# Linear and multi-query attention, forward and gradient: where padding is zeroed, how a column of k sums is spread, and how the last dK products are placed

## The chip, the cores and the metric

The kernel runs on one core of a Trainium2 chip. Its time is the device time of one execution in microseconds, taken as the median of several runs. The profile is that of one further execution. Five engines work side by side, each with its own queue of instructions in a fixed order: TensorE (PE, with its weight loads shown apart as PEld), VectorE (DVE), ScalarE (ACT), GpSimd (POOL) and SyncE (SP). ACT, POOL and SP also issue DMA transfers from their queues, so an instruction that waits holds up the transfers behind it.

## What is computed

The reference joins two attention blocks side by side, on sequences of 2048 with 448 features and 16 heads of 28, and returns the output together with the gradients of all eight inputs. The kernel therefore computes a forward and a backward pass of both:

```python
def _A_ref(x, wqkv, wo):                      # linear attention
    q, k, v = heads(x @ wqkv)                 # (1, 16, 2048, 28) each
    phi = lambda t: jnp.where(t > 0, t + 1, jnp.exp(t)) + 1e-6
    pq, pk = phi(q), phi(k)
    kv = jnp.einsum("bhsd,bhse->bhde", pk, v)
    z = jnp.einsum("bhsd->bhd", pk)           # the sums over k
    num = jnp.einsum("bhqd,bhde->bhqe", pq, kv)
    den = jnp.einsum("bhqd,bhd->bhq", pq, z)[..., None] + 1e-6
    return merge(num / den) @ wo

def _B_ref(x, wq, wk, wv, wo):                # softmax attention, one k and one v for all heads
    q, k, v = heads(x @ wq), x @ wk, x @ wv
    p = softmax(jnp.einsum("bhqd,bkd->bhqk", q, k) * Dh ** -0.5)
    return merge(jnp.einsum("bhqk,bkd->bhqd", p, v)) @ wo

_out, _vjp = jax.vjp(forward, A_x, A_wqkv, A_wo, B_x, B_wq, B_wk, B_wv, B_wo)
return (_out, *_vjp(grad_out))
```

(`heads` and `merge` stand for the reshapes and transposes of the reference, which are cut here.)

## The kernel before

The sequence is cut into 16 tiles of 128 rows, the features into chunks of 128, 128, 128 and 64 rows. Everything is held in SBUF between the stages. There are three stages.

**Phase A, the linear attention** (`phase_A`), with its order made by a scheduler that interleaves what the code writes one after the other. It uses PSUM tiles of two names, four buffers each: "agen" for short products and "aacc" for accumulators. Its short-lived SBUF tiles come from the pool `awk` under three names: "osb" (three buffers, evicted results on their way to an output), "phiT" (three) and "pr" (two, f32).

- K, V and the k sums: `k1acc` collects x^T phi(k) over the tiles, and since columns 448 to 463 of x are ones (line 151), its rows 64 to 79 of chunk 3 hold the k sums. `hilo` (line 246) splits it into two bf16 parts `K1T`, line 284 transposes them by DMA into `K1`, and line 287 keeps the negated sums by head in `zrow`. Line 355 takes the column of sums out of the transposed `K1`, spreads it over the heads and masks it: `Zm`, which `den` (line 328) multiplies with phi(q).
- The gradient of wqkv: `gw` (line 429) accumulates x^T g over all tiles into four aacc banks, ACT copies three of them into osb tiles (line 444), ACT and DVE add the two halves of the fourth (lines 441 and 442, the sum in a fourth osb tile), and POOL issues the stores (line 445). It is called at line 450 and again at line 520.
- Between lines 419 and 427 the transposed weights `wqT` and `wkT` are brought by DMA, and POOL zeroes the unused half of their last chunk (line 422, "MEMSET ga"). POOL's queue holds this beside its copies of line 426, the stores of `gw` and the zeroing of `wo_pr` (line 467).
- After the first `gw` a product over the 16 tiles (lines 451 to 457) fills agen tiles that DVE evicts (line 457); POOL's and SyncE's loads for the next stage follow it. The loop of line 477 writes two outputs for each of four chunks through osb tiles (lines 481 and 491). The last product of the phase (line 525) needs `gkT`, which SyncE transposes at line 476.

**The main loop** (lines 911 to 1021) has its order written out by hand: `manual_schedule`, 512 steps u and 28 to empty the pipeline. A step computes two tiles of scores S (`rows_SD`), their exponentials (lines 940 and 986), dP (banks `DB`), dS (lines 952 to 955), and some steps later O and dQ (`o_dq`), dV (`dv_mm`) and dK (`dk_m`, line 855). A `dk_m` call issues four matmuls of 32x32 weights and 512 columns, on the four array tiles of the diagonal, (32a, 32a), into the one bank `dk_acc`. At odd u four of them are issued together. From u = 512 on there are no more scores; in the steps that remain, inputs of the drain are loaded (`post_load`, line 757), the gradient of wo is accumulated in spare banks (`gwo`, line 781, at even u from 520), and the last two tiles of the output projection are done (u = 532 and 536, in the bank `spare`). `post_load(8)` brings the padded weight `wqT`, and POOL then issues 14 small transfers that patch rows of it (`PADS`, line 770). At u = 531 SyncE transposes the finished dQ into `dqn`, in a tile of the name dsx (line 1011).

**The drain** (from line 1036), again ordered by the scheduler. dV and dK are copied into `dkvT` (lines 1036 to 1044; ACT and DVE take turns for dK), 14 small transfers patch rows of dQ^T (`qT_B`) with rows of `dkvT`, shared between SyncE and POOL (line 1083), `dwq` and `dkv_T` prepare weight gradients, and `dx` (line 1071) multiplies the patched dQ^T with the patched `wqT`. Results leave through `sbuf()`, a ring of five tiles of the name dsT.

Of the kernel before, what the change touches and what calls it, by code (L numbers as in the profile page):

```python
# [14 lines left out]
H = 16  # L15
# [10 lines left out]
def kernel(  # L26
# [61 lines left out]
    def flat(t):  # L88
        return t.rearrange("p a b -> p (a b)")
# [34 lines left out]
    def phase_A(pa, cA, cB, awk, psA):  # L124
# [157 lines left out]
        hilo(K1T, k1acc)  # L282
        for i in range(2):
            nc.sync.dma_start_transpose(K1[i][:].rearrange("p c h k -> p (c h) k"), flat(K1T[i]))
        for st in range(NS - LAG, NS):
            qproj(st)
        nc.vector.tensor_tensor(out=zrow[64:80, :], in0=k1acc[3][64:80, :], in1=mrow[64:80, :], op=ALU.mult)
# [67 lines left out]
        nc.vector.tensor_tensor(out=Zm[:], in0=hm[:], in1=K1[0][:, 3, :, 64:65].to_broadcast([P, 4, H]), op=ALU.mult)  # L355
# [65 lines left out]
        for t in (wqT, wkT):  # L421
            nc.gpsimd.memset(t[64:128, 3, :], 0.0)
# [6 lines left out]
        def gw(gn, blk):  # L429
# [6 lines left out]
            for c in range(4):  # L436
                r = DC_ROWS[c]
                sb = awk.tile([P, 512], BF16, name="osb")[:, 0:D]
                if c == 3:
                    odd = awk.tile([P, H, DH], F32, name="pr", bufs=2).rearrange("p h e -> p (h e)")[0:64, :]  # L440
                    nc.scalar.activation(out=odd, in_=al[3][64:128, :], func=ACT.Copy)
                    nc.vector.tensor_tensor(out=sb[0:64, :], in0=al[3][0:64, :], in1=odd, op=ALU.add)  # L442
                else:
                    nc.scalar.activation(out=sb[0:r, :], in_=al[c][0:r, :], func=ACT.Copy)
                g_ = nc.gpsimd.dma_start(out_2[c * P:c * P + r, blk * D:(blk + 1) * D], sb[0:r, :])
# [4 lines left out]
        gw(gqn, 0)  # L450
# [26 lines left out]
        for i in range(4):  # L477
# [13 lines left out]
            sb = awk.tile([P, 512], BF16, name="osb")[:, 0:D]  # L491
# [155 lines left out]
    with ExitStack() as cs_:  # L647
# [109 lines left out]
        def post_load(k):  # L757
# [8 lines left out]
            if k == 8:  # L766
                post["wqT"] = t[:, 0:4 * D].rearrange("p (g c) -> p g c", c=D)
                nc.sync.dma_start(post["wqT"], wqT_d[:, :].rearrange("(g p) c -> p g c", p=P))
                for g, r, c in PADS:
                    nc.gpsimd.dma_start(post["wqT"].rearrange("(j r) g c -> j r g c", r=32)[:, r, g, :], wkvT_d[c:c + 4, :])  # L770
# [24 lines left out]

        GW = [0, 0, 4, 4, 10, 10, 16, 16, 22, 22, 28, 28, 34, 34, 40, 40, 48, 48, 56, 56, 64, 64]
# [58 lines left out]
        def dk_m(b, m):  # L855
            qc, pair, g, hp = blk(b)
            h, B, s = m // 8, (m // 2) % 4, m % 2
            for a in range(4):
                rhs = dsx[b][32 * a:32 * a + 32, :, h, :, :].rearrange(
                    "p u t (b i s) -> p u t b i s", b=4, s=2)[:, :, :, B, :, s]  # L860
                mmt(dk_acc[32 * a:32 * a + 32, :],
                    qX[qc][32 * a:32 * a + 32, B, s, pair * 64 + 32 * h:pair * 64 + 32 * h + 32],
                    rhs, (32 * a, 32 * a), b == 0 and m == 0, b == NB - 1 and m == 15)
# [47 lines left out]
        with tc.manual_schedule():  # L911
# [8 lines left out]
            for u in range(NU + 28):  # L920
# [5 lines left out]
                spare = SB[(2 * u + 2) % 3] if hasS else SB[2]  # L926
# [66 lines left out]
                if u % 2:  # L993
                    b, i = divmod(u - 27, 8)
                    if 0 <= b < NB:
                        for m in range(2 * i, 2 * i + 4):
                            dk_m(b, m)
# [7 lines left out]
                if 512 <= u < 530 and u % 2 == 0:  # L1005
                    post_load((u - 512) // 2)
                if u == 531:
                    dqn = px_.tile([P, 8, 2, 2, 256], BF16, name="dsx").rearrange("p a b c d -> p (a b c d)").rearrange(
                        "p (t d) -> p t d", d=512)
                    for g_ in range(4):  # L1010
                        nc.sync.dma_start_transpose(dqn[:, :, g_ * P:(g_ + 1) * P], qT_B[g_])
# [24 lines left out]
        for c in range(4):  # L1036
            nc.vector.tensor_copy(out=dkvT[32:64, c * 512:(c + 1) * 512], in_=dv_acc[32 * c:32 * c + 32, :])
        for c in range(4):
            t = dkvT[0:32, :].rearrange("p (t a i) -> p t a i", a=4, i=32)[:, :, c, :]
            src = dk_acc[32 * c:32 * c + 32, :].rearrange("p (t i) -> p t i", i=32)  # L1040
            if c % 2:
                nc.vector.tensor_scalar(out=t, in0=src, scalar1=scale, scalar2=None, op0=ALU.mult)
            else:
                nc.scalar.activation(out=t, in_=src, func=ACT.Copy, scale=scale)

        def dwq(c):
            r = DC_ROWS[c]
            al = gen(0)
            for st in range(NS):
                rhs = dqn[:, st, :].rearrange("p (h c) -> p h c", c=32)[:, :, 1:1 + DH]  # L1050
# [84 lines left out]
```

## Time and profile before

| what | value |
|---|---|
| runs | 1065.06, 1064.52, 1064.60 us; median 1064.6 us |
| profiled execution | 1065.64 us, of which span 1063.9 us |
| busy: PE | 1013.7 us (95% of the span) |
| busy: DVE | 899.6 us (85%) |
| busy: ACT | 869.6 us (82%) |
| busy: POOL | 781.7 us (73%) |
| mean granted clock of TensorE | 0.998 |

The span is the stretch from the first to the last instruction in the profile; the run's time includes what lies around it. A busy share is a mean over the stages, and a PE shown as busy is not PE at its peak. A line of the order of time gives start, duration, engine, source line, operation, what it writes and reads, and in brackets how long its engine idled before it and who ended that. Inside a helper every matmul has the helper's line (81 for `mm`, 672 for `mmt`, 85 for `half_mm`), so the tile names tell which product it is.

The page's rows by slices of the span (40 equal ones, busy in tenths) show where the engines pause:

```
PE   9999799998999999999999999999999999999998
DVE  6897410569999999999999999999999999999942
ACT  6463032589999999999999999999999999999522
POOL 6001152228898998899889988989998988888881
```

### The profile page before, as it was taken

What the parts mean: (1) busy time and instruction counts of PE and PEld (TensorE: products, weight loads), DVE (VectorE), ACT (ScalarE), POOL (GpSimd) and SP (SyncE); (2) the same over time, 40 slices, a digit from 0 to 9 for tenths busy, and PEclk for the clock granted to TensorE, in tenths of its full rate; (3) what the DMA queues carried; (4) which work ended last, traced back from release to release, by engine and by line L of the source; (5) the groups of instructions that cost most, each with busy time, mean ns of one, the idle gap of its engine ahead of it and who ended that gap; (6) DMA issues with size and microseconds to landing.
All of it is one profiled execution on the core that took longest, in us unless ns stands there. A gap on an engine that the chain in (4) does not pass through costs nothing.

```text
span 1063.9 us, 40030 instructions
## 1 busy us (share of the span) xinstructions
PE 1013.7 (95%) x16232; PEld 487.2 (46%) x16241; DVE 899.6 (85%) x1799; ACT 869.6 (82%) x1739; POOL 781.7 (73%) x1034
## 2 busy tenths in 40 slices
PE   9999799998999999999999999999999999999998
PEld 5555355434444444444444444444444444444444
DVE  6897410569999999999999999999999999999942
ACT  6463032589999999999999999999999999999522
POOL 6001152228898998899889989988998989888881
PEclk9999999999999999999999999999999999999999
DMA  9879899179999999999999999999999999999963
GB/s 263 152 128 188 165 210 233 36 138 200 192 184 196 192 186 196 199 185 177 207 195 192 185 201 189 191 199 198 193 190 179 200 186 193 202 187 178 228 135 89
DMA packets 689937, 195.15 MB, mean 183 GB/s; under 512 B 670616, under 2 KB 687792, under 8 KB 689752
## 3 DMA queue, kind: packets, MB, share of 16 engines
q1 hardware_dynamic: 680152, 179.92, 101.9%
q0 software_dynamic: 4640, 8.71, 2.9%
q10 hardware_dynamic: 4960, 3.96, 1.3%
q8 instruction: 127, 2.08, 0.8%
q14 instruction: 58, 0.48, 0.2%
HBM read 12.60 MB, written 10.84 MB: 22 GB/s over the span
## 4 chain that ended last, share of the span: by engine, by line
PE 44%; ACT 32%; issue 13%; DVE 4%; POOL 4%; DMA 2%; ACTq 0%; DVEq 0%; SPq 0%; POOLq 0%
ACT cp L954 16%; ACT eT L986 13%; PE agen L81 12%; PE agen L672 11%; PE aacc L672 10%; PE aacc L81 7%; POOL dsT L955 3%; PE aacc L806 2%; ACT eT L940 2%; PE aacc L837 1%; DVE dsx L1019 1%; DVE dsT L952 1%; DMA dsx<-R 1%; DMA pk<-in_B_x_dram 1%; DMA out_dram<-osb 1%
## 5 line engine op out<-in xcount | busy, mean ns | idle before, releaser
L955 POOL TENSOR_TENSOR dsT<-cp,eT 128x512 bf16<-128x512 bf16 x512 | 588.3, 1157 | 77.0 <-ACT cp L954 70.6
L1019 DVE STREAM_TRANSPOSE dsx<-dsT 128x512 f32<-128x512 f32 x512 | 357.8, 699 | 4.1 <-POOL dsT L955 1.9
L672 PEld LDWEIGHTS <-R 32*128 32x128 bf16 (+1 forms) x9104 | 227.7, 94 | 275.4 <-issue 239.7
L952 DVE TENSOR_TENSOR dsT<-agen,eT 128x512 bf16<-128x512 f32 x512 | 341.9, 668 | 10.5 <-PE agen L672 5.4
L940 ACT ACTIVATE eT<-aacc 128x512 bf16<-128x512 f32 x512 | 313.1, 612 | 15.3 <-PE agen L672 6.0
L954 ACT ACTIVATE cp<-agen 128x512 bf16<-128x512 f32 x512 | 314.8, 615 | 12.6 <-PE agen L672 11.2
L986 ACT ACTIVATE eT<-aacc 128x512 bf16<-128x512 f32 x512 | 320.8, 627 | 0.0
L672 PE MATMUL agen<-dsx,qX 32*32 32x512 bf16 x4096 | 267.7, 375 | 0.0
L672 PE MATMUL agen<-doT,R 32*128 32x256 bf16 x2048 | 246.7, 269 | 3.0 <-DVE dsT L952 1.4
L672 PE MATMUL aacc<-R,R 32*128 32x256 bf16 (+1 forms) x2240 | 218.1, 268 | 8.1 <-DVE oTs L816 3.2
L672 PE MATMUL agen<-eT,R 128*32 128x256 bf16 x2048 | 158.0, 274 | 0.2 <-issue 0.2
L672 PE MATMUL agen<-dsT,R 128*32 128x256 bf16 x2048 | 157.0, 274 | 0.1
L672 PEld LDWEIGHTS <-qX 32*32 32x32 bf16 x4096 | 79.7, 89 | 113.9 <-issue 53.3
L672 PE MATMUL aacc<-eN,don 128*32 128x512 bf16 x1024 | 96.9, 379 | 0.0
L81 PEld LDWEIGHTS <-R 128*128 128x128 bf16 x517 | 41.3, 99 | 50.2 <-issue 19.3
L426 POOL COPY pk<-R 128x256 bf16<-128x256 bf16 x4 | 1.6, 400 | 64.1 <-DVE R L386 64.0
L81 PE MATMUL agen<-R,R 128*128 128x448 bf16 (+1 forms) x174 | 41.1, 360 | 1.5 <-ACT R L229 0.8
L848 POOL COPY qst<-R 128x512 bf16<-128x512 bf16 x56 | 34.3, 612 | 6.5 <-DMA qX<-qst 6.5
L820 POOL TENSOR_TENSOR prod<-R,oTs 128x128 f32<-128x128 bf16 x64 | 27.6, 432 | 9.3 <-DVE oTs L816 9.3
L672 PEld LDWEIGHTS <-don 128*32 128x32 bf16 x1024 | 33.9, 97 | 0.8 <-issue 0.3
L442 DVE TENSOR_TENSOR osb<-aacc,pr 64x448 bf16<-64x448 f32 x2 | 1.2, 616 | 36.7 <-DMA out_dram<-osb 36.7
L971 DVE TENSOR_SCALAR R<-agen 64x256 bf16<-64x256 f32 x64 | 27.3, 427 | 3.6 <-PE agen L672 1.6
(229 smaller groups left out, 959.2 us busy)
## 6 DMA issues: line engine op xcount, KB each, us to landing
out_dram<-osb ACTq DMA_DIRECT2D x22, 112.0 KB
eN<-eT SPq DMA_TRANSPOSE x128
xa<-in_A_x_dram SPq DMA_DIRECT2D x8, 224.0 KB
ga<-in_grad_out_dram SPq DMA_DIRECT2D x4, 448.0 KB
xa<-in_grad_out_dram POOLq DMA_DIRECT2D x4, 448.0 KB, 7.1
out_dram<-wdq POOLq DMA_DIRECT2D x8, 224.0 KB, 5.0
eT<-in_grad_out_dram SPq DMA_DIRECT2D x4, 448.0 KB
eT<-in_B_x_dram SPq DMA_DIRECT2D x4, 448.0 KB
```

What stands on the lines that cost most here:

```text
L81: nc.tensor.matmul(out_ap, lhsT=lhsT, rhs=rhs, start=start, stop=stop, tile_position=(0, 0))
L672: nc.tensor.matmul(out, lhsT=lhsT, rhs=rhs, start=start, stop=stop, tile_position=pos, skip_group_check=True)
L806: nc.tensor.transpose(onp[:, qb, :, :].rearrange("p h c -> p (h c)"), oTs[0:64, qb * P:(qb + 1) * P], identF[0:64, 0:64], tile_position=(0 ...
L820: nc.gpsimd.tensor_tensor(out=prod[b][:], in0=dnv, in1=os_, op=ALU.mult)
L848: eng.tensor_copy(out=st.rearrange("p (b s) a j -> p b s a j", s=2)[:, :, s, :, :], in_=src.unsqueeze(2).to_broadcast([P, 4, 4, 32]))
L940: nc.scalar.activation(out=eT(u)[:, 0, :], in_=sp[0][:, :], func=ACT.Exp, scale=scale)
L952: nc.vector.tensor_tensor(out=dst[:, 0, :], in0=dp[0][:, :], in1=ew[:, 0, :], op=ALU.mult)
L954: nc.scalar.activation(out=cp[:, :], in_=dp[1][:, :], func=ACT.Copy)
L955: nc.gpsimd.tensor_tensor(out=dst[:, 1, :], in0=cp[:, :], in1=ew[:, 1, :], op=ALU.mult)
L971: nc.vector.tensor_scalar(out=qT_B[g][64 * hp:64 * hp + 64, qc * 256:(qc + 1) * 256], in0=oq[64:128, 0:256], scalar1=scale, scalar2=None, ...
L986: nc.scalar.activation(out=eT(u)[:, 1, :], in_=sp[1][:, :], func=ACT.Exp, scale=scale)
L1019: nc.vector.transpose(out=dsx[b][:, tp, :, :, :].rearrange("p h t c -> p (h t c)").bitcast(F32), in_=dsT[y][:, :, :].rearrange("p h c -> p ...
```

## The change

In phase A: `zrow` is computed right after `hilo`; `Zm` comes from four small matmuls of `K1T` with columns of the identity, read from PSUM, where it was read from the transposed `K1`; the zeroing of `wqT` and `wkT` is issued behind the last store of the first `gw`; the fourth result of `gw` uses a tile of the name pr, and one of the two outputs of the loop of line 477 uses phiT, so that six buffers serve where there were three.

In the drain: at the odd steps from u = 519 to 535 every second `dk_m` goes to the array tiles (32a, 32((a + 2) mod 4)) and into a second bank, `SB[2]`, which ACT copies to SBUF at u = 536 and which DVE adds when it scales dK into `dkvT`. dV is copied to `dkvT` by ACT at u = 533. `dqn` lies in two tiles of the ring eN and is transposed in eight halves at u = 523 to 531. The padded weight is loaded at u = 526, and its 14 patches are issued by SyncE at u = 532.

```diff
@@ phase A
         hilo(K1T, k1acc)
+        nc.vector.tensor_tensor(out=zrow[64:80, :], in0=k1acc[3][64:80, :], in1=mrow[64:80, :], op=ALU.mult)
...
             qproj(st)
-        nc.vector.tensor_tensor(out=zrow[64:80, :], in0=k1acc[3][64:80, :], in1=mrow[64:80, :], op=ALU.mult)
...
-        nc.vector.tensor_tensor(out=Zm[:], in0=hm[:], in1=K1[0][:, 3, :, 64:65].to_broadcast([P, 4, H]), op=ALU.mult)
+        zs = gen([P, 4, H])
+        for c in range(4):
+            mm(zs[:, c, :], K1T[0][:, 3, c * P:(c + 1) * P], identB[:, 64:64 + H])
+        nc.vector.tensor_tensor(out=Zm[:], in0=zs[:], in1=hm[:], op=ALU.mult)
...
-        for t in (wqT, wkT):
-            nc.gpsimd.memset(t[64:128, 3, :], 0.0)
...
-                sb = awk.tile([P, 512], BF16, name="osb")[:, 0:D]
                 if c == 3:
+                    sb = awk.tile([P, H, DH], F32, name="pr", bufs=2).rearrange("p h e -> p (h e)").bitcast(BF16)[:, 0:D]
...
                 else:
+                    sb = awk.tile([P, 512], BF16, name="osb")[:, 0:D]
...
-        gw(gqn, 0)
+        with tc.issue_after(gw(gqn, 0).ins):
+            for t in (wqT, wkT):
+                nc.gpsimd.memset(t[64:128, 3, :], 0.0)
...
-            sb = awk.tile([P, 512], BF16, name="osb")[:, 0:D]
+            sb = awk.tile([P, D], BF16, name="phiT")
             nc.scalar.activation(out=sb[0:r, :], in_=ps[0:r, 0:D], func=ACT.Copy)
@@ main loop and drain
-                for g, r, c in PADS:
-                    nc.gpsimd.dma_start(post["wqT"].rearrange("(j r) g c -> j r g c", r=32)[:, r, g, :], wkvT_d[c:c + 4, :])
...
+        dqn = [by_tokens(flat(ENs[(124 + c) % 6])) for c in range(2)]
...
-        def dk_m(b, m):
+        dk_two = SB[2]
+
+        def dk_m(b, m, other=0):
...
-                mmt(dk_acc[32 * a:32 * a + 32, :],
+                k = 32 * ((a + 2) % 4) if other else 32 * a
+                mmt((dk_two if other else dk_acc)[k:k + 32, :],
                     qX[qc][32 * a:32 * a + 32, B, s, pair * 64 + 32 * h:pair * 64 + 32 * h + 32],
-                    rhs, (32 * a, 32 * a), b == 0 and m == 0, b == NB - 1 and m == 15)
+                    rhs, (32 * a, k), other == 2 or b == 0 and m == 0, other == 0 and b == NB - 1 and m == 15)
...
-                spare = SB[(2 * u + 2) % 3] if hasS else SB[2]
+                spare = SB[(2 * u + 2) % 3] if hasS else DB[u // 4 % 2] if u > 530 else SB[2]
...
-                            dk_m(b, m)
+                            dk_m(b, m, (1 + (u == 519 and m == 2 * i + 1)) * (m % 2) if 519 <= u < 537 else 0)
...
-                if 512 <= u < 530 and u % 2 == 0:
+                if 512 <= u < 528 and u % 2 == 0:
                     post_load((u - 512) // 2)
-                if u == 531:
...
-                        nc.sync.dma_start_transpose(dqn[:, :, g_ * P:(g_ + 1) * P], qT_B[g_])
+                if u == 526:
+                    post_load(8)
+                if u == 532:
+                    for g, r, c in PADS:
+                        nc.sync.dma_start(post["wqT"].rearrange("(j r) g c -> j r g c", r=32)[:, r, g, :], wkvT_d[c:c + 4, :])
+                for v, half, gs in ((523, 0, (0, 1)), (525, 0, (2, 3)), (527, 1, (0, 1)), (529, 1, (2,)), (531, 1, (3,))):
+                    for g_ in gs if u == v else ():
+                        nc.sync.dma_start_transpose(dqn[half][:, :, g_ * P:(g_ + 1) * P],
+                                                    qT_B[g_][:, half * 1024:half * 1024 + 1024])
+                if u == 533:
+                    for c in range(4):
+                        nc.scalar.activation(out=post["dkvT"][32:64, c * 512:(c + 1) * 512], in_=dv_acc[32 * c:32 * c + 32, :],
+                                             func=ACT.Copy)
+                if u == 536:
+                    dk_sum = pd_.tile([P, 2, 512], BF16, name="dsT").rearrange("p a b -> p (a b)").bitcast(F32)
+                    for c in range(2):
+                        r = 64 * (1 - c)
+                        nc.scalar.activation(out=dk_sum[64 * c:64 * c + 64, :], in_=dk_two[r:r + 64, :], func=ACT.Copy,
+                                             scale=scale)
...
         for c in range(4):
-            nc.vector.tensor_copy(out=dkvT[32:64, c * 512:(c + 1) * 512], in_=dv_acc[32 * c:32 * c + 32, :])
-        for c in range(4):
             t = dkvT[0:32, :].rearrange("p (t a i) -> p t a i", a=4, i=32)[:, :, c, :]
             src = dk_acc[32 * c:32 * c + 32, :].rearrange("p (t i) -> p t i", i=32)
-            if c % 2:
-                nc.vector.tensor_scalar(out=t, in0=src, scalar1=scale, scalar2=None, op0=ALU.mult)
-            else:
-                nc.scalar.activation(out=t, in_=src, func=ACT.Copy, scale=scale)
+            nc.vector.scalar_tensor_tensor(out=t, in0=src, scalar=scale,
+                                           in1=dk_sum[32 * c:32 * c + 32, :].rearrange("p (t i) -> p t i", i=32),
+                                           op0=ALU.mult, op1=ALU.add)
...
-                rhs = dqn[:, st, :].rearrange("p (h c) -> p h c", c=32)[:, :, 1:1 + DH]
+                rhs = dqn[st // 8][:, st % 8, :].rearrange("p (h c) -> p h c", c=32)[:, :, 1:1 + DH]
```

More of the change, by code (lines that the diff above doesn't have):

```diff
@@ L1003 @@
                 y = u - 18
-                if 512 <= u < 530 and u % 2 == 0:
+                if 512 <= u < 528 and u % 2 == 0:
                     post_load((u - 512) // 2)
-                if u == 531:
-                    dqn = px_.tile([P, 8, 2, 2, 256], BF16, name="dsx").rearrange("p a b c d -> p (a b c d)").rearrange(
-                        "p (t d) -> p t d", d=512)
-                    for g_ in range(4):
-                        nc.sync.dma_start_transpose(dqn[:, :, g_ * P:(g_ + 1) * P], qT_B[g_])
+                if u == 526:
[17 more added lines that the diff above has]
+                                             scale=scale)
                 if u >= 519:
```

## The prediction

> **What bounds the kernel now.** I read the page's busy shares first (PE 95%, DVE 85%, ACT 82%), then the queue of PE stalls ahead of the main loop, then the order of time around the two stages that the diff touches. From 250 to 985 us the built order of every engine is the same in both kernels, and that loop is left out. What counts is the linear-attention stage (0 to 216 us) and the drain (989 us to the end). The waits of PE before 240 us, as (us in total, times, longest):
>
> ```profile
> PE agen L81 <- DVE wdq L457: 5.4, 1, 5.4
> PE aacc L81 <- DVE zrow L287: 1.4, 1, 1.4
> PE aacc L81 <- DVE blks L301: 0.6, 1, 0.6
> PE agen L81 <- ACT osb L492: 0.3, 1, 0.3
> ```
>
> PE is fed without a gap elsewhere in this stage, so these few waits are nearly all that can be won there. The order of time around the largest (start, duration, engine, line, idle before it and its releaser):
>
> ```profile
> 113.66 3.20 PE L81 MATMUL agen<-KOT,R 128*128 128x448 bf16 x16
> ...
> 117.68 0.47 POOL L422 MEMSET ga<- 64x448 bf16 x1 [14.40 <-DMA ga<-R]
> 118.25 1.64 POOL L445 DMA_DIRECT2D out_dram<-osb  x3
> ...
> 121.10 0.62 DVE L442 TENSOR_TENSOR osb<-aacc,pr 64x448 bf16<-64x448 f32 x1 [16.04 <-DMA out_dram<-osb]
> ...
> 122.30 8.00 PE L81 MATMUL agen<-KOT,R 128*128 128x448 bf16 x33 [5.44 <-DVE wdq L457]
> ```
>
> The chain reads backwards: PE has filled its four agen banks and waits for DVE; DVE stands at L442 since it needs one of three osb buffers; that buffer's store stands in POOL's queue behind the memset L422; and the memset waits for SyncE's transposes (ga<-R). The stretch after it has a second price. Columns: stretch, its length, busy of PE, PEld, DVE, ACT, POOL, granted clock, DMA share, GB/s:
>
> ```profile
> 116.90:122.30 5.40, 0.00 (x1) 0.00 (x0) 1.20 (x3) 0.00 (x0) 4.21 (x6) 0.99 0.70 161
> 122.30:125.60 3.30, 3.30 (x10) 1.28 (x10) 2.94 (x9) 0.00 (x0) 0.26 (x1) 0.50 0.39 88
> 125.70:131.50 5.80, 5.80 (x33) 2.97 (x31) 5.54 (x16) 0.00 (x0) 0.00 (x0) 1.00 0.81 177
> ```
>
> After the idle 5.4 us the granted clock is 0.50 for 3.3 us. In the drain:
>
> ```profile
> 1002.31 0.39 PE L672 MATMUL agen<-doT,R 32*128 32x256 bf16 x4
> 1002.63 1.05 PE L672 MATMUL agen<-dsx,qX 32*32 32x512 bf16 x16
> 1003.61 0.39 PE L672 MATMUL agen<-doT,R 32*128 32x256 bf16 x4
> ...
> 1029.95 1.69 PE L81 MATMUL aacc<-eT,R 128*128 128x448 bf16 x8
> 1032.30 4.43 PE L81 MATMUL aacc<-dsx,eT 128*128 128x448 bf16 x21 [0.66 <-DMA dsx<-R]
> ```
> ```profile
> 1002.73 0.69 DVE L952 TENSOR_TENSOR dsT<-agen,eT 128x512 bf16<-128x512 f32 x1 [0.40 <-PE agen L672]
> ```
> ```profile
> 1016.04 7.87 POOL L770 DMA_DIRECT2D eT<-wkvT_d  x14 [0.29 <-issue]
> ```
>
> From 1001 us to 1031.6 us PE starts each group where the last one ends (one gap of 0.44), and DVE waits for PE: PE sets the pace. A dK group of 16 takes 0.98 us, from its start to the next one's.
>
> **Part 1, the blocked store.** In the new order of POOL the three stores and the memset of wo_pr come before the zeroing, and L442's sum goes into a pr buffer. The 5.44 us wait of PE goes. DVE then needs 0.72 us for each of the 16 tiles (L457 starts at 127.28, 128.00, 128.72), PE 0.75 (4 matmuls at 0.19), so PE stays just ahead as the bound. PE's 64 matmuls now run from 113.66 to 132.97, 19.3 us; at the undisturbed 0.19 each they take 12.1. Gain 7.2 us, of which 5.4 is the wait and 1.8 the half clock. What is late next: SyncE's queue. It stood until 121.77 for wo_pr's memset and is then busy without a break to 168 us. It is free from 118.30 (end of pq<-pk), so it gains only 3.5 us. Its first product that PE needs is gkT, issued at 137.87, read by PE at 155.60. Shifted, that is 134.4 against 148.4, still 14 us of room for an issue of 3.5. The moved memsets need transposes landed at 117.68, and their first reader on PE (wkT, in the last product) comes at about 148. Behind them on POOL stand only the loads of wst, which wait for PE anyway until 125.8. Bounds: 3.5 (all PE work hangs on SyncE) and 7.2; with 14 us of room I take 7.2.
>
> **Part 2, six output buffers.** ACT waits at L482 and L492 for stores five times (0.24 to 2.06 us), but PE only 0.28. Gain 0.3, from 0 to 0.3. The second L442 waits 20.7 us with no reader near: nothing.
>
> **Part 3, zrow and Zm.** PE's 1.38 us wait for L287 and the 0.57 for L301 stand before a DVE that never pauses from 42.2 to 51.7 us, so moving 0.62 us of it forward only reorders the queue. In the new order the first L301 ends near 49.8 instead of 50.6 and the last three at the same 51.3. PE gains at the first kv_blk and loses it again at the second; what is left are DVE's pauses, 0.28 and 0.15. Four matmuls of 16 columns are added (16 of them took 0.40 us, so 0.1) and hide in the old wait. Zm's read moves from SBUF to PSUM, 0.21 against 0.23 (L339, same size): nothing. The old Zm never waited for its transpose. Gain 0.4; bounds 0 and 1.9 (both waits).
>
> **Part 4, dK on eight tiles.** Nine groups change (odd u from 519 to 535); each keeps 16 matmuls and 16 weight loads, but odd m go to a second bank and other array tiles. The trace shows four such matmuls of 512 columns at a time, 0.245 us per four; eight at a time isn't shown. Nearest row: dQ and O, four tiles on the same rows with different data, 16 matmuls and 16 loads in 0.55 us, 17 ns an instruction, so issuing isn't the limit. Bounds for a group: 0.98 (no overlap gained) and 0.49; I take 0.50, so up to 0.48 each. Where dP products follow (u = 521, 523, 525) the next one needs DVE's L952: it starts 0.42 after the group before and lasts 0.69, so PE could go on at 1003.48 instead of 1003.61. Gain 0.13 x 3 = 0.4. At u = 519 DVE paces already: 0. For u = 527, 529, 531, 533, 535 PE is alone: 5 x 0.48 = 2.4. Sum 2.8, from 0 to 4.3 (nine full groups). PE's wait at 1019.59 for L791 stays.
>
> [...]
>
> Merging dK: two ACT copies (about 0.6 each, nearest L1044's 0.59) run at u = 536, where ACT idles 3.8 us. After the loop the chain ACT, DVE, ACT, DVE (1030.07 to 1032.72) becomes four DVE operations at some 0.65: 2.6, the same, and PE reads dkvT only 4.3 us after its dwq start.
>
> **Part 5, dqn and the patches.** dqn is transposed from u = 523 on; the 0.66 us that PE waits at 1032.30 goes. In the new order four dwq(1) matmuls stand first and cover ACT's copy of SB[1]. SyncE takes the 14 patches at u = 532: 14 x 0.5 (L1083's 0.497) = 7 us behind the last transpose, which waits for DVE's L971 (1018.11, now 1.5 or so earlier) and needs 1.5: they end near 1026. Behind them stand seven qT_B patches; four need dkvT's dK rows, ready near 1029.8, so SyncE has 3 us of room. POOL sheds 7.87 us. Its last three qT_B patches wait behind four out_8 stores: ready 1029.6, 7 issues at 0.55 = 1033.4, plus 2.2 to land (3.6 the longest seen) = 1035.6 to 1037.0; PE's dx starts at 1039.69 - 2.8 - 0.66 = 1036.2 and reads the last of them about a us later. Just enough; without that cover it costs up to 1. Gain 0.66, from -0.4 to 0.66.
>
> **Sum.** 7.2 + 0.3 + 0.4 + 2.8 + 0.7 = 11.4. The profiled span is 1063.9 (its run 1065.64); the median of the runs is 1064.6, 0.7 over the span. So span 1052.5, time 1053.2.
>
> **Rivals.**
> A: eight tiles gain nothing. For it: S and dP, where tiles on different rows share the columns as the new pairs do, take 0.48 for 8 matmuls of 256 columns, less than two at a time. Against: these load 128 weight columns for each matmul, dK and dQ 32, and dQ is the nearer row. Parts 1, 2, 3 and 5 remain: 8.6, time 1056.0.
> B: SyncE's queue takes over after part 1. For it: it is busy from 121.77 to 168 without a break. Against: the 14 us of room. Part 1 is then 3.5: 7.7 in all, time 1056.9.
> C, the other side: tiles that share rows shut each other out, and a changed group runs one matmul after the other, 16 x 0.216 (448 columns take 0.19) = 3.46 instead of 0.98. Nine groups cost 22.3; less the 8.6 gained elsewhere 13.7 is lost, time 1078.3. It decides from 1.94 us a group on (8.6 / 9 = 0.96 more). Against it: the four column tiles of dQ share all rows and keep 0.11 us per four.
> D: the reordering of part 3 wins both waits: 1051.7.
>
> **How the numbers follow.** Forecast 0.56, A 0.18, B 0.11, C 0.04, D 0.06; 0.05 for a stall that I don't see (0.03 of it faster all the same, 0.01 no change, 0.01 slower). Within 0.2% (2.1 us) counts as no change, about what a measurement here can tell. Faster: 0.56 + 0.18 + 0.11 + 0.06 + 0.03 = 0.94, same 0.01, slower 0.05. The forecast's own range is 1051.7 (part 4 at its 4.3) to 1055 (part 4 at half, part 5's cover gone). With the rivals it is 1050.2 (part 3's and part 4's upper ends together, 3.0 less) to 1057.6 (B with the 0.7 of dqn lost), which leaves out C and the unseen.
>
> **What would show it.** Right: no PE wait above 1 us near 114 to 126, the clock there at 1.00, and the product's 64 matmuls in 12 us; the main loop starting 7.9 earlier; dK groups of about 0.5 us from u = 527 on and a wait of PE for L952 at u = 521 to 525; dwq without a wait for dqn. Wrong: a wait for gkT or for SyncE's loads, dK groups at 0.98 or above, or PE standing before dx for a patch (part 5's cover gone).

## The result, and the profile after

| | runs, us | median | ratio to before, with 95% interval |
|---|---|---|---|
| before, on the same chip | 1061.13 to 1065.06 (6) | 1064.36 | |
| changed | 1055.19, 1056.07, 1059.91, 1060.22, 1058.50, 1058.07 | 1058.28 | 0.9945 [0.9925, 0.9964] |
| predicted | 1050.2 to 1057.6 | 1053.2 | |

The change is faster by 6.1 us where 11.4 were forecast, and its runs lie 5 us apart. The profiled execution is the fastest of them (1055.19 us, span 1053.5), so it shows what the change can give, and the rest has to be looked for in other executions. The waits of PE over the whole span, the ones that answer to those of before, read (us in total, times, longest):

```profile
PE agen L81 <- ACT phiT L496: 2.9, 1, 2.9
PE aacc L81 <- DVE blks L301: 1.4, 2, 1.1
```

The 5.4 us wait for DVE's L457 (now L461) is gone, and so is the one for zrow, which came back as a longer wait for L301. But a wait of 2.9 us that before had at 0.3 stands on top of the list. The order of time around it, first PE, ACT and SyncE (start, duration, engine, line, idle before it and who ended that):

```profile
112.52 12.28 PE L81 MATMUL agen<-KOT,R 128*128 128x448 bf16 x64
135.07 1.46 PE L81 MATMUL agen<-ga,blks 128*128 128x512 bf16 x6 [2.86 <-ACT phiT L496]
148.50 0.93 PE L81 MATMUL agen<-KO,pq 128*128 128x448 bf16 x4
```
```profile
129.43 0.54 ACT L486 ACTIVATE osb<-agen 128x448 bf16<-128x448 f32 x1 [2.55 <-PE agen L313]
134.04 0.34 ACTq L487 DMA_DIRECT2D out_dram<-osb  x1
134.48 0.55 ACT L496 ACTIVATE phiT<-agen 128x448 bf16<-128x448 f32 x1 [4.50 <-DMA pk<-in_B_x_dram]
```
```profile
117.67 0.94 SPq L474 DMA_DIRECT2D R<-in_B_wo_dram  x2
118.72 2.15 SPq L115 DMA_TRANSPOSE pk<-in_B_x_dram  x1
...
128.21 1.03 SPq L474 DMA_DIRECT2D R<-in_B_wo_dram  x2
129.34 2.48 SPq L115 DMA_TRANSPOSE pk<-in_B_x_dram  x1
```

The 64 matmuls now run in 12.28 us without a wait, as forecast. Behind them ACT has copied the first result at 129.97, but issues its store (L487) only at 134.04, and the copy queued behind that store (L496) names its releaser: not a result of PE, but SyncE's last transpose of x (pk<-in_B_x). PE has by then filled its banks and waits for L496. In the trace L487 waits, besides for its own copy, on the DMA semaphore that this transpose (issued at 129.34) signals at 133.77 to 133.96; SyncE's 21 issues from 117.67 to 134.66 take eight such semaphores in one order, and the store has the next in that order. In the kernel before the same store (there L483) stood until 139.09 for the same reason, a transpose issued at 132.50 that signals up to 139.02, but PE came 8 us later and lost only 0.3:

```profile
137.77 0.55 ACT L482 ACTIVATE osb<-agen 128x448 bf16<-128x448 f32 x1 [2.55 <-PE agen L313]
139.09 0.35 ACTq L483 DMA_DIRECT2D out_dram<-osb  x1
139.55 0.55 ACT L492 ACTIVATE osb<-agen 128x448 bf16<-128x448 f32 x1 [1.24 <-DMA pk<-in_B_x_dram]
```

The granted clock through these 64 matmuls, the new wait and the matmuls after it (stretch, length, busy of PE, PEld, DVE, ACT, POOL, clock, DMA share, GB/s):

```profile
112.52:124.64 12.12, 12.12 (x67) 6.28 (x65) 11.44 (x29) 0.54 (x1) 3.78 (x6) 1.00 0.85 169
132.20:135.07 2.87, 0.02 (x1) 0.00 (x0) 0.00 (x0) 0.59 (x2) 2.31 (x10) 1.00 0.77 178
135.07:138.40 3.33, 3.33 (x22) 1.83 (x22) 0.00 (x0) 1.37 (x3) 2.45 (x6) 1.00 0.93 192
```

The half clock of before (0.50 for 3.3 us) is gone from the first row, and in this execution the new wait brings none: the clock is 1.00 in all three. The drain:

```profile
1014.94 0.41 PE L676 MATMUL agen<-dsx,qX 32*32 32x512 bf16 x4
1014.95 0.41 PE L676 MATMUL aacc<-dsx,qX 32*32 32x512 bf16 x4
1015.18 0.40 PE L676 MATMUL agen<-dsx,qX 32*32 32x512 bf16 x4
1015.20 0.40 PE L676 MATMUL aacc<-dsx,qX 32*32 32x512 bf16 x4
1015.53 0.93 PE L81 MATMUL agen<-wo,R 128*128 128x448 bf16 x4
...
1018.88 1.69 PE L81 MATMUL aacc<-eT,R 128*128 128x448 bf16 x8
1020.41 4.21 PE L81 MATMUL aacc<-eN,eT 128*128 128x448 bf16 x20
```

The groups of eight tiles overlap pair by pair (agen is the old bank, aacc the second one) and take 0.59 us from start to the next group's start; dwq follows at 1020.41 without the wait for dqn.

### The profile page after: what moved, and what is told of

It is laid out like the page before. It is cut to its first block, busy times and chain, and to the rows that moved or that the text cites. A ratio compares the mean times of both kernels' runs of the same rounds, so it can differ in the third digit from the quotient of the medians.

```text
span 1053.5 us, 40033 instructions
## 1 busy us (share of the span) xinstructions
PE 1008.2 (96%) x16245; PEld 485.7 (46%) x16245; DVE 898.1 (85%) x1797; ACT 871.2 (83%) x1743; POOL 772.8 (73%) x1020
## 4 chain that ended last, share of the span: by engine, by line
PE 43%; ACT 33%; issue 14%; DVE 5%; POOL 3%; DMA 1%; ACTq 0%; DVEq 0%; SPq 0%; POOLq 0%
ACT cp L960 17%; ACT eT L992 13%; PE agen L81 13%; PE aacc L676 10%; PE agen L676 10%; PE aacc L81 6%; POOL dsT L961 2%; ACT eT L946 2%; PE aacc L809 2%; PE aacc L840 1%; DVE dsT L958 1%; DVE dsx L1039 1%; DMA pk<-in_B_x_dram 0%; DMA out_dram<-dsT 0%; PE aacc L85 0%
## 5 line engine op out<-in xcount | busy, mean ns | idle before, releaser
L958 DVE TENSOR_TENSOR dsT<-agen,eT 128x512 bf16<-128x512 f32 x512 | 341.7, 667 | 10.3 <-PE agen L676 5.1
L960 ACT ACTIVATE cp<-agen 128x512 bf16<-128x512 f32 x512 | 314.9, 615 | 11.4 <-PE agen L676 10.3
L676 PE MATMUL agen<-dsx,qX 32*32 32x512 bf16 x4024 | 264.1, 376 | 0.0
L81 PEld LDWEIGHTS <-R 128*128 128x128 bf16 x517 | 40.9, 98 | 41.9 <-issue 11.8
```

The costliest lines, as they stand in the source:

```text
L81: nc.tensor.matmul(out_ap, lhsT=lhsT, rhs=rhs, start=start, stop=stop, tile_position=(0, 0))
L676: nc.tensor.matmul(out, lhsT=lhsT, rhs=rhs, start=start, stop=stop, tile_position=pos, skip_group_check=True)
L958: nc.vector.tensor_tensor(out=dst[:, 0, :], in0=dp[0][:, :], in1=ew[:, 0, :], op=ALU.mult)
L960: nc.scalar.activation(out=cp[:, :], in_=dp[1][:, :], func=ACT.Copy)
```

## The span cut into stretches

To compare executions I cut every profile at five instructions that all kernels have: the first of the 64 matmuls, the first matmul of the phase's final product (agen<-KO,pq behind `gw`), the first and the last product oTs of DVE in the main loop, and the first matmul of dwq. The numbers are differences of their start times, in us; "wait" is PE's wait for L496 in all (in the kernels with osb there, for that copy). "To the end" is what is left of the span, which is read to 0.1 us.

| kernel | to the 64 matmuls | to the final product | wait | to the loop | loop | to dwq | to the end | span |
|---|---|---|---|---|---|---|---|---|
| before, 1st profile | 113.66 | 40.60 | 0.3 | 74.37 | 764.53 | 39.14 | 31.60 | 1063.9 |
| before, 2nd (d1) | 113.01 | 42.47 | 0.9 | 74.36 | 763.41 | 38.86 | 31.99 | 1064.1 |
| before, 3rd (d2) | 113.08 | 41.75 | 2.1 | 74.36 | 763.69 | 39.25 | 31.37 | 1063.5 |
| changed, 1st | 112.52 | 35.98 | 2.9 | 74.36 | 761.42 | 36.13 | 33.09 | 1053.5 |
| changed, 2nd (a1) | 113.47 | 40.21 | 4.8 | 74.36 | 762.87 | 36.12 | 32.77 | 1059.8 |
| changed, 3rd (d3) | 112.70 | 36.54 | 3.4 | 74.36 | 762.85 | 36.09 | 32.86 | 1055.4 |
| a2 Wo loads by POOL | 112.94 | 36.92 | 2.1 | 74.37 | 760.13 | 36.09 | 31.95 | 1052.4 |
| a3 zeroing first | 113.33 | 40.32 | 5.1 | 74.36 | 761.46 | 36.09 | 32.44 | 1058.0 |
| b4 three buffers | 113.27 | 36.87 | 3.3 | 74.36 | 764.02 | 36.09 | 32.69 | 1057.3 |
| b3 both of these | 113.48 | 41.27 | 1.4 | 74.36 | 763.49 | 36.11 | 32.39 | 1061.1 |
| b1 stores by POOL | 113.67 | 32.97 | 0 | 74.57 | 763.17 | 36.24 | 32.18 | 1052.8 |
| b2 stores and Wo by POOL | 113.32 | 32.96 | 0 | 74.37 | 761.68 | 36.11 | 31.66 | 1050.1 |
| c1 before, stores by POOL | 115.09 | 41.90 | 2.3 | 74.36 | 765.08 | 39.49 | 31.38 | 1067.3 |
| d4 before, parts 1 and 2, stores by POOL | 115.17 | 32.97 | 0 | 74.56 | 762.91 | 39.08 | 31.31 | 1056.0 |
| a4 dK on four tiles | 113.47 | 38.16 | 3.4 | 74.36 | 761.90 | 38.33 | 32.48 | 1058.7 |
| c2 dqn late | 113.35 | 37.33 | 2.9 | 74.36 | 763.74 | 37.46 | 34.86 | 1061.1 |

## The experiments

Every median is compared with that of before, measured beside it (1065.33 for a1 to a4, 1066.40 for b1 to b4, 1065.36 for c1 and c2, 1065.40 for d1 to d4); before itself thus moves by 1.1 us. An interval behind a ratio is its 95% interval.

**The changed kernel again (a1, d3).** No edit.

> The changed kernel unaltered, to see what of its profile comes back. Theory (ACT's held store): the 2.86 us in which PE waited at 132 us for ACT's eviction of the first product of out_3 stands in every execution and grows where SyncE's last transpose of x lands later, up to the 5.4 us of before with its half clock; so the profile shows it at 3 to 6 us, the stretch from there to the end of the loop keeps the 761.4 us (first to last oTs product on DVE, 222.86 to 984.28), and the median is 1056 to 1059. Rival (the loop): the wait is 2.9 us again, and the loop takes 762 to 766 us as in the kernel before (764.5), so that what the first profile showed beyond the edits (3.1 us) was that execution's own.

> The changed kernel unaltered, a third profile. Theory: PE's wait for ACT's first eviction of out_3 is there again, 2.8 to 5.2 us; the stretch from the 64 matmuls to the final product is 36 to 40.3 us, and the span follows it. Rival (2.86 and 4.83 were outliers): no wait over 1 us, the stretch 33 us.

Measured: a1 1061.28 us median (1058.64 to 1063.42), ratio 0.9954 [0.9936, 0.9973]; d3 1057.08 (one run). PE's wait in a1, and the clock around it:

```profile
136.97 0.34 ACTq L487 DMA_DIRECT2D out_dram<-osb  x1
137.41 0.54 ACT L496 ACTIVATE phiT<-agen 128x448 bf16<-128x448 f32 x1 [6.48 <-DMA pk<-in_B_x_dram]
...
138.00 2.72 PE L81 MATMUL agen<-ga,blks 128*128 128x512 bf16 x6 [4.83 <-ACT phiT L496]
```
```profile
133.10:138.00 4.90, 0.07 (x2) 0.00 (x0) 0.00 (x0) 0.59 (x2) 3.27 (x14) 0.77 0.82 149
138.00:141.40 3.40, 3.40 (x14) 1.72 (x14) 0.00 (x0) 1.36 (x3) 0.11 (x1) 0.50 0.93 198
```

The six matmuls of 512 columns took 1.46 us in the first profile and take 2.72 here: with the longer wait the half clock that part 1 had removed is back. The stretch is 4.2 us longer than in the first profile and the span 6.3, and the median lies 2.3 above the expected 1056 to 1059. The wait is there in all three profiles of the changed kernel. The rival was not excluded, since the loop also takes 1.5 us more than in the first profile.

**Wo's rows loaded by POOL (a2).**

```diff
-            nc.sync.dma_start(wo_pr[32 * j + 1:32 * j + 1 + DH, g, 0:D], B_wo[h * DH:(h + 1) * DH, :])
+            nc.gpsimd.dma_start(wo_pr[32 * j + 1:32 * j + 1 + DH, g, 0:D], B_wo[h * DH:(h + 1) * DH, :])
```

> The sixteen loads of Wo's rows go by POOL's queue in place of SyncE's, so that SyncE's four transposes of x follow each other from 118 us and land some 7 us earlier than 134. Theory (ACT's held store): ACT issues its first store right after the eviction at 130, PE's wait of 2.86 us goes, the final product of the first phase starts at about 145.6 in place of 148.5, and the time falls by 2.9 us or more against the changed kernel's median of the same call, with a smaller spread. Rival (the wait's owner is another, or SyncE's next product takes it over): the start of the final product moves by less than 0.5 us and the time stays within 1 us. POOL issues 16 more transfers at some 0.55 us each from 117.6, in a stretch in which it waited for PE.

Measured: 1053.92 us (1052.09 to 1063.31), ratio 0.9899 [0.9869, 0.9929]. ACT and PE:

```profile
130.42 0.34 ACTq L487 DMA_DIRECT2D out_dram<-osb  x1
...
135.48 0.34 ACTq L487 DMA_DIRECT2D out_dram<-osb  x1
135.92 0.54 ACT L496 ACTIVATE phiT<-agen 128x448 bf16<-128x448 f32 x1 [4.08 <-DMA gaT<-wdq]
```
```profile
136.51 1.02 PE L81 MATMUL agen<-ga,blks 128*128 128x512 bf16 x4 [2.12 <-ACT phiT L496]
137.37 10.93 PE L81 MATMUL aacc<-wdq,xa 128*128 128x448 bf16 x48
```

Three transposes of x now go out by 123.43, and the first store goes at 130.42, at once; the second goes at 135.48 only, and the copy behind it names as its releaser SyncE's next product (gaT<-wdq, a transpose of gkn issued at 125.50). The theory's cause stands, but the stretch is 36.92 us where 33.1 were expected (from 112.52 to 145.6): the wait moved to the next store and is 2.12 us, with a half clock behind it (0.50; 10.93 us for the 48 matmuls that take 9.24 in the first profile). The spread did not get smaller either, with one run at 1063.31. The time fell by 7.4 us against a1, of which this stretch gives 3.3; the loop and the end are 2.7 and 0.8 shorter in this profile. Whether that belongs to the edit is not shown; the short end is seen again in b2, which has the same edit (last section).

**Parts 1 and 2 taken back, one at a time and together (a3, b4, b3).** a3 puts the zeroing back ahead of the stores:

```diff
+        for t in (wqT, wkT):
+            nc.gpsimd.memset(t[64:128, 3, :], 0.0)
         pkT = v4(pq)
...
-        with tc.issue_after(gw(gqn, 0).ins):
-            for t in (wqT, wkT):
-                nc.gpsimd.memset(t[64:128, 3, :], 0.0)
+        gw(gqn, 0)
```

b4 keeps that and takes osb for all four results of `gw` and for out_3 again; b3 does both.

```diff
-                if c == 3:
-                    sb = awk.tile([P, H, DH], F32, name="pr", bufs=2).rearrange("p h e -> p (h e)").bitcast(BF16)[:, 0:D]
+                sb = awk.tile([P, 512], BF16, name="osb")[:, 0:D]
+                if c == 3:
...
-            sb = awk.tile([P, D], BF16, name="phiT")
+            sb = awk.tile([P, 512], BF16, name="osb")[:, 0:D]
```

> The zeroing of the two transposed weights goes back to its old place, ahead of the stores of the first product of out_2; everything else stays changed. Theory: the wait of 5.4 us and the half clock behind it come back ahead of the 64 matmuls (12.3 to about 14 us), but SyncE's queue then is in time for ACT's stores, so the 2.9 us go: slower than the changed kernel by 7.2 - 2.6 = 4.6 us in profiles. Rival (part 1 keeps its full price): slower by 7.2. Second rival (it was never worth more than the median shows): by 3 or less.

> Parts 1 and 2 both taken back (zeroing ahead of the stores, three output buffers), parts 3 to 5 stay. Putting the zeroing back alone had brought back 0.27 us of the 5.4 us wait. Theory (either edit alone removes that wait, and SyncE's held stores eat most of it): here the 5.4 us wait and the half clock come back, the x48 matmuls take 10.8 us again, but the wait for ACT's eviction is under 0.5; the time is 1 to 4 us above the changed kernel's 1061.3. Rival (the wait's removal is worth its full price): 7 us above, about 1068.

> Part 2 alone taken back (three output buffers, the zeroing stays behind the stores). Theory: no wait over 0.3 us in the 64 matmuls, the wait for ACT's eviction of out_3 at 3 to 5.5 us as in the changed kernel, the time within 1.5 us of its 1061.3. Rival (the buffers carry it): the 5.4 us wait comes back.

Measured: a3 1060.48 us, 0.9957 [0.9939, 0.9974]; b4 1060.17, 0.9927 [0.9899, 0.9955]; b3 1061.07, 0.9951 [0.9931, 0.9972]. The 64 matmuls in a3, then in b3, behind the wait (the view ends at 125 us, inside them):

```profile
121.34 3.94 PE L81 MATMUL agen<-KOT,R 128*128 128x448 bf16 x20 [0.27 <-DVE wdq L461]
```
```profile
121.45 3.89 PE L81 MATMUL agen<-KOT,R 128*128 128x448 bf16 x11 [4.77 <-DVE wdq L460]
```

a3 was expected to bring the 5.4 us back and brought 0.27: with the sum of L442 in a buffer of its own, DVE no longer needs the blocked store, so the place of the zeroing does not matter. With three buffers but the new place (b4) the wait is 0.24. Only with both taken back (b3) is it there. Either edit alone does the work of part 1. And the time hardly sees it: all three are within 1.2 us of a1's 1061.3, since b3, which loses 4.77 us in the 64 matmuls, then waits only 1.4 behind ACT's store, while a3 and b4 lose almost nothing there and wait 5.1 and 3.3. That is the give-back, in one column of the table. It was expected that a3 would be 4.6 us slower than the changed kernel, and b3 1 to 4 us; neither is slower at all. Against the three profiles of the changed kernel (mean 37.6) b3's stretch of 41.3 is 3.7 longer, so the medians alone don't measure what parts 1 and 2 are worth; c1 and d4 below do.

**ACT's stores by POOL (b1), and with Wo's loads too (b2).**

```diff
-            nc.scalar.dma_start(out_2[i * P:i * P + r, 2 * D:3 * D], sb[0:r, :])
+            nc.gpsimd.dma_start(out_2[i * P:i * P + r, 2 * D:3 * D], sb[0:r, :])
...
-            nc.scalar.dma_start(out_3[i * P:i * P + r, :], sb[0:r, :])
+            nc.gpsimd.dma_start(out_3[i * P:i * P + r, :], sb[0:r, :])
```

> The eight stores of the loop that makes the k part of out_2 and out_3 are issued by POOL in place of ACT; the loads of Wo stay on SyncE's queue. Theory (PE waits because ACT's evictions stand behind ACT's own stores, which wait for SyncE's transfers): from the end of the 64 matmuls to the start of the final product PE needs 21.0 us, without a wait over 0.5, against 23.9 in the changed kernel's first profile, 28.1 in its second and 24.8 with the loads of Wo on POOL; the time is 4 to 7 us below the changed kernel's 1061.3, about 1054 to 1057. Rival (a transfer that PE itself needs is late): the wait moves to another instruction of the same stretch and the stretch stays over 23 us.

> Both: the eight stores and the sixteen loads of Wo by POOL. Theory: the stretch from the 64 matmuls to the final product is 21.0 us as with the stores alone, since PE hangs on neither any more; the time equals that run's within 1 us. Rival (SyncE's transposes are late for the final product once the stretch is 3 to 7 us shorter): then this one, whose transposes go out earlier, is faster than the stores alone by 1 us or more. POOL's own work grows by 24 issues of some 0.55 us, 13 us in a stretch in which it stood idle 15; if that is too much, the loads of xa behind it are late and PE waits after 150 us.

Measured: b1 1054.51 us (1052.69 to 1056.86), 0.9879 [0.9850, 0.9909]; b2 1052.62 (1051.74 to 1056.99), 0.9868 [0.9840, 0.9896], the best kernel here. ACT and PE in b1:

```profile
131.19 0.54 ACT L496 ACTIVATE phiT<-agen 128x448 bf16<-128x448 f32 x1
131.70 0.54 ACT L486 ACTIVATE osb<-agen 128x448 bf16<-128x448 f32 x1
```
```profile
131.45 1.46 PE L81 MATMUL agen<-ga,blks 128*128 128x512 bf16 x6
132.74 0.63 PE L313 MATMUL agen<-R,K 128*128 128x140 bf16 x8
133.21 1.46 PE L81 MATMUL agen<-ga,blks 128*128 128x512 bf16 x6
```

PE runs through. From the 64 matmuls to the final product it needs 32.97 us, where before needed 40.60 in the profile that the forecast was made from: 7.6 us, against the 7.2 and 0.3 of parts 1 and 2. b1's span of 1052.8 is that of the forecast's sum (1052.5) only by luck: its loop is 1.4 us shorter than before's, which the forecast left out, and that stands in for what the drain, the end and part 3 fell short of. The rival for b2 was that SyncE's transposes are late for the final product; the stretch is the same to 0.01 us with and without Wo's loads, so this mechanism falls. But b2's median is 1.9 us lower, where the theory had them within 1 us; their runs overlap, and what this difference is stays open.

**The kernel before with the stores by POOL (c1), and with parts 1 and 2 as well (d4).** The edits are those shown, on the kernel before.

> The kernel before with one edit: the eight stores of the k part of out_2 and of out_3 by POOL in place of ACT, parts 1 to 5 all absent. Theory (two waits in a row, of which the first hides the second): PE's wait of 5.4 us in the 64 matmuls stays, ACT's held store had cost PE only 0.3, so the stretch from these matmuls to the final product stays at 40 to 40.6 us and the time within 1 us of before; only with parts 1 and 2 does the store's queue matter, and with it they give 7.6. Rival (ACT's stores cost the kernel before as well): faster by 2 us or more.

> The kernel before with parts 1 and 2 and the eight stores by POOL, without parts 3, 4 and 5. Theory: the 64 matmuls run without a wait and so does the stretch behind them, 33.0 us in place of 40.6; the time is 7.6 us below before's 1065.4, 1057 to 1059. Rival (what is won there is lost later in the loop or at the end): less than 5 us below.

Measured: c1 1067.32 us, ratio 1.0020 [1.0003, 1.0037]; d4 1057.21, 0.9915 [0.9892, 0.9937]. In c1 (the first row again as far as 125 us):

```profile
122.97 2.32 PE L81 MATMUL agen<-KOT,R 128*128 128x448 bf16 x6 [4.67 <-DVE wdq L457]
...
145.32 1.02 PE L81 MATMUL agen<-ga,blks 128*128 128x512 bf16 x4 [2.26 <-ACT osb L492]
```
```profile
144.72 0.54 ACT L492 ACTIVATE osb<-agen 128x448 bf16<-128x448 f32 x1 [4.58 <-DMA out_dram<-osb]
```

Moving the stores alone wins nothing: it was expected within 1 us and is 2 slower, and the stretch is 41.9 us where 40 to 40.6 were expected, with a wait of ACT, and behind it of PE, at the osb ring of three. With parts 1 and 2 it takes 8.2 us off before's median, the expected 7.6 within the spread, and the stretch is 32.97 us without a wait. So parts 1 and 2 and the place of the stores bring their full price only together.

**dK on four tiles again (a4), dqn late again (c2).** In a4 `dk_m(b, m)` is called without its third argument, `dk_sum` is left out, and ACT and DVE take turns in scaling dK as before. In c2:

```diff
-        dqn = [by_tokens(flat(ENs[(124 + c) % 6])) for c in range(2)]
...
+                if u == 531:
+                    dqn = px_.tile([P, 8, 2, 2, 256], BF16, name="dsx").rearrange("p a b c d -> p (a b c d)").rearrange(
+                        "p (t d) -> p t d", d=512)
+                    for g_ in range(4):
+                        nc.sync.dma_start_transpose(dqn[:, :, g_ * P:(g_ + 1) * P], qT_B[g_])
```

> All groups of dK in the drain on four array tiles again, without the second accumulator and its merge; everything else stays changed. Theory: the groups of 16 matmuls take 0.98 us in place of 0.55, waits of 0.2 us go in three rounds, so the drain is 2.8 us longer (bounds 2.0 to 3.0) and so is the time. Rival (the eight tiles gained nothing on the path, other engines set the rounds): the drain from the last products of the loop to the first product of dwq changes by less than 0.5 us.

> The changed kernel with dqn as before: one tile of the dsx buffers, four transposes of 2048 columns at u = 531, ahead of the patches on SyncE's queue. Theory: PE's wait ahead of dwq, 0.66 us in the kernel before, comes back and is longer by what the eight tiles have shortened the drain (2.2 us by the run with four tiles), so 2 to 3.5 us; the stretch from the last oTs product to dwq's first matmul is 38 to 39.6 us in place of 36.1, and the time is 1.5 to 3.5 us above the changed kernel's 1061.3. Rival (transposes issued in time, part 5 worth its 0.66 or less): 36.1 to 36.8 us. A wait for the patches ahead of dx would show behind it, up to 1 us, since they now stand behind the longer transposes.

Measured: a4 1062.23 us (0.9971 [0.9958, 0.9985]), c2 1063.17 (0.9979 [0.9962, 0.9997]). In a4 a group takes 0.98 us again, from its start to the next product's:

```profile
1014.79 1.05 PE L676 MATMUL agen<-dsx,qX 32*32 32x512 bf16 x16
1015.77 0.93 PE L81 MATMUL agen<-wo,R 128*128 128x448 bf16 x4
```

The stretch to dwq is 2.2 us longer (38.33 against 36.12): less than the expected 2.8, within its bounds. The median is only 1.0 above a1's, where the same 2.8 were expected; the runs of both spread by some 5 us. In c2:

```profile
1026.24 4.22 PE L81 MATMUL aacc<-dsx,eT 128*128 128x448 bf16 x20 [1.22 <-DMA dsx<-R]
...
1035.54 0.35 PE L81 MATMUL aacc<-eT,R 128*128 128x448 bf16 x1 [1.75 <-DMA R<-eN]
```

The first wait is under the expected 2 to 3.5, and the patches behind the long transposes cost more than the expected 1: 1.22 before dwq and 1.75 before dx. Together 3.0 us, 1.9 in the medians.

**The kernel before again (d1, d2).** No edit.

> The kernel before, unaltered, for a second profile. The stretch from the first to the last oTs product of the main loop took 764.5 us in its first profile and 760.1 to 764.0 in nine profiles of kernels with parts 3 to 5, though every engine's instructions in it are the same in the same order. Theory (the loop varies by itself from execution to execution): one of the two new profiles of before falls under 763. Rival (something in the change makes the loop shorter by about 2 us): both stay at 764 to 766. The 64 matmuls to the final product: 40 to 41 us with the wait of 4.7 to 5.5, every time.

> A third profile of the kernel before, as the second: theory and rival the same. From dwq's first matmul to the end 31.2 to 31.8 us if the 31.6 of the first profile is the kernel's own, against 31.7 to 33.1 in the changed ones.

Measured: 1065.84 and 1065.15 us. The loop took 763.41 and 763.69 us, between the two expectations: five profiles of kernels without parts 3 to 5 give 762.9 to 765.1 (mean 763.9), eleven with them 760.1 to 764.0 (762.4). The ranges overlap and the order of instructions in the loop is the same, so whether the 1.5 us belong to the change stays open. The stretch behind the 64 matmuls' start varies too, more than expected (42.47 and 41.75 us for 40 to 41), and so does the wait for ACT's copy in it (0.9 and 2.1 us).

## Why the prediction was wrong, step by step

**Part 1, the step that failed.** The mechanism was right to the end of the 64 matmuls. What failed is the question of what is late next: "Its first product that PE needs is gkT, issued at 137.87, read by PE at 155.60 ... still 14 us of room". SyncE's first transfer that PE hangs on is not gkT but the last transpose of x, and not through PE's operands: ACT's store waits for it, the next copy waits behind the store, and PE waits for the bank. The trace of before has that store at 139.09, and part 2 priced all of ACT's waits there by PE's 0.28 us, as they stood, without shifting PE by 7 us against them. Of the 7.5 us of parts 1 and 2, three profiles each of before and after give 4.0 (mean 41.6 to 37.6), and between 0.4 and 6.5 for single pairs. The bound of 3.5 that I named ("all PE work hangs on SyncE") was close to this, and rival B, at 1056.9, was nearer to the medians than the forecast; its place was right, its path was not. With the stores on another queue the full 7.6 come out (b1, b2, d4). The main loop, forecast to start 7.9 us earlier, starts 4.4 earlier in the mean of three.

**Part 2.** Named at 0.3, for PE's wait for ACT's copy. That did not come: the wait is 2.9 to 4.8 us with six buffers and 3.3 with three (b4). What part 2 does is to remove the same wait as part 1 (a3), so the two are one gain, counted once in the sum, under part 1.

**Part 3.** Forecast 0.4. From the 16 matmuls at 42 us to the 64 matmuls the three profiles of before need 71.02, 71.02 and 71.09, those of the changed kernel 70.80, 70.83 and 70.95: 0.2. But in c1 and d4, which have before's code there, the old wait is followed by a half clock:

```profile
50.00:52.00 2.00, 1.43 (x15) 1.32 (x13) 1.54 (x8) 0.00 (x0) 0.00 (x0) 0.68 1.03 194
52.00:54.00 2.00, 2.00 (x21) 2.00 (x19) 0.58 (x3) 0.00 (x0) 0.00 (x0) 0.50 1.12 206
```

These rows are d4's; it and c1 reach the 64 matmuls at 115.1 to 115.2 us, all others at 112.5 to 113.7. The three profiles of before and the eleven with part 3 don't show this, so part 3 is worth 0.2 us or some 1.6, by the execution (the last section has waits of like length that went either way).

**Part 4.** The mechanism and the count were right (PE waits 0.2 us for L958 three times, as forecast for u = 521 to 525). The size was off: a group takes 0.59 us, not 0.50, so the five free groups give 5 x 0.39 = 1.95, and with the 0.4 that is 2.3; a4 shows 2.2 against the 2.8 forecast. The 0.50 took the overlap of the pairs as nearly full, and it is a little less than that. On four tiles and one bank the 16 matmuls take 0.98 us in a4 too, on eight tiles and two banks 0.59, the pairs overlapping.

**Part 5.** Forecast 0.66. Before's mean of 39.08 to dwq against a4's 38.33 gives 0.75, and no patch is waited for. With the shorter drain of the changed kernel it is worth more, 3.0 in c2, late patches included.

**The end and the offset.** From dwq to the end the changed kernel takes 32.9 us (mean of three), before 31.7: some 1.3 us are given back, which no part foresaw (below). And span and run lie 1.7 us apart in both kernels (1055.19 over 1053.5, 1065.64 over 1063.9); the 0.7 of the forecast set the span of one execution against the median of others, which leaves the gain of 11.4 as it was. The upper end of the forecast's own range doesn't follow from its terms: part 4 at half (1.4 less) and part 5 at its lower end (1.06 less) make 1055.7, not 1055.

**The sum.** By means of three profiles: 0.4 up to the 64 matmuls, 4.0 behind them, 1.5 in the loop, 3.0 up to dwq, less 1.3 at the end: 7.6, as the spans have it (1063.8 to 1056.2). The medians have 6.1 and 4.1.

## What to carry to other kernels

When a wait of one engine goes, shift that engine's whole later order by the gain and hold every other engine's old instant against it; a stall that cost 0.3 us before can be worth all of the gain (here it came to 2.9 to 4.8 of 7.5). An engine that evicts for PE should not also issue stores whose turn can depend on another queue's transfers: here eight stores moved to another queue shortened the stretch by 4.6 us in the mean, and the edits that made them matter by 4.0. Where runs spread by more than the step in question, cut several profiles at the same instructions before believing one.

## What the runs showed of the hardware

**A store's issue waits for another engine's transfer.** Here the choice of the issuing engine counts by what its issues wait for: ACT's first store stood 4.1 us (129.97 to 134.04) in the first profile and 6.0 in a1 (130.93 to 136.97), for a transfer that SyncE had issued, and the same eight stores on POOL shorten the stretch from 37.6 (mean of three) to 33.0 us.

**A half clock followed some waits and not others of like length.** During or right after waits of PE of 2.12 (a2), 2.92 (c2), 3.36 (a4), 4.83 (a1) and 5.13 us (a3) the granted clock fell to 0.50, after 2.86 (changed), 3.33 (b4) and 3.41 us (d3) it did not. In before's first profile the half clock lasts 3.41 us, from 122.16 to 125.57, and in the 3.41 us ahead of it (118.74 to 122.16) PE has no matmul; in the 3.41 us ahead of those (115.33 to 118.74) PE idles 1.88, and the clock stays at 1.00. The first record of the clock there starts at 6.10 us, and the half clock 34 times 3.413 us later. In a2 it also lasts 3.41 us, in a1 some 6.9 (worked out from the clocks of a1's rows above). So I cut two other profiles into stretches of that length, counted from their first record of the clock: two in a row of a2, then two of d3 (columns as above):

```profile
134.35:137.76 3.41, 1.29 (x9) 0.59 (x7) 0.00 (x0) 0.98 (x2) 2.90 (x9) 1.00 1.04 213
137.76:141.18 3.42, 3.42 (x11) 1.38 (x10) 0.00 (x0) 0.52 (x2) 3.30 (x6) 0.50 1.15 314
130.49:133.90 3.41, 1.91 (x17) 1.10 (x15) 0.00 (x0) 0.00 (x0) 2.64 (x9) 1.00 1.00 187
133.90:137.31 3.41, 1.50 (x10) 0.79 (x10) 0.00 (x0) 1.51 (x4) 2.04 (x9) 1.00 0.57 134
```

In a2 the whole wait of 2.12 us lies in one stretch, and the next one runs at half clock; in d3 the longer wait is shared by two, 1.50 and 1.91 us of idle PE, and the clock stays (1.00 from 137 to 150 us too). In these rows of before, a2 and d3, half clock follows a stretch with 3.41 and with 2.12 us of idle PE, and none follows 1.50, 1.88 or 1.91. That the place of a wait among such stretches decides is my reading of them; no run was made to test it.

**The end is 0.4 to 1.2 us longer after the change.** From the start of the last eviction on DVE to the end it is 3.3 to 3.4 us in all five profiles without parts 3 to 5, and 3.7 to 4.5 in the eleven others: 3.7 in a2 and b2, the two with Wo's loads on POOL, and 4.1 to 4.5 in the other nine. In the queue table of the last 20 us, the changed kernel's profile has three packets of instruction transfers on queue 14 where before's has one (queue and kind: packets, MB, share of the 16 engines):

```profile
q14 instruction: 3, 0.02, 0.6%
```

and its last 2 us carry 8 GB/s at a time when the outputs are done (columns as in the stretches above):

```profile
1051.50:1053.50 2.00, 0.00 (x0) 0.00 (x0) 0.00 (x0) 0.00 (x0) 0.00 (x0) 0.62 0.02 8
```

Two of the three start in the last 1.0 us (at 1052.53 and 1053.49); before's one starts at 1044.32, 19.6 us from its end. Over the whole span that queue has 59 packets in the changed kernel, 58 in before and 58 in b2. So a fetch of the last instructions would account for 0.4 to 0.8 us of the longer end, the 4.1 to 4.5 us less the 3.7. That is an argument from what goes together in three profiles; it wasn't tried, and the other 0.4 us are unexplained.
